# One gated-recurrence attention and max-of-two MLP kernel: two stages in sequence rewritten as one software pipeline by groups of 512 tokens

## The chip, the cores and the metric

The kernel runs on one core of one Trainium2 chip. The metric is the device time of a run in microseconds (us); before the change the median of three runs is 328.61 us (328.46 to 329.25).

## The reference

Attention: for 4 batches, 8 heads, 768 positions and a head size of 48, a 48x48 state is decayed and updated at each position, and the output reads it.

```python
f = 1.0 / (1.0 + np.exp(-f_logit))
for t in range(S):
    state = f[:, :, t, :, None] * state + np.einsum('bhd,bhe->bhde', k[:, :, t], v[:, :, t])
    y[:, :, t] = np.einsum('bhd,bhde->bhe', q[:, :, t], state)
x = attn_out.transpose(0, 2, 1, 3).reshape(B * S, H * D)      # 3072 tokens x 384
h1 = x @ w1                                                   # w1, w2: 384 x 1024
h2 = x @ w2
out = np.maximum(h1, h2) @ w_out                              # w_out: 1024 x 384
```

## The kernel before

The recurrence is computed in chunks of 128 positions. An outer loop runs over the 6 chunks, an inner one over the 4 batches, so there are 24 steps, and a step handles 128 tokens of all 8 heads. In a step, three DMAs on SyncE (SP) and one on GpSimd (POOL, with a cast to bf16; line 81) bring q, k, f and v in runs of 48 numbers. ScalarE (ACT) makes `ell = ln(1 + exp(-f))` (lines 90 and 91). TensorE (PE) sums it along the chunk with a triangular matrix (`cumL`, line 94) and per head (line 112). ACT takes two exponentials of the sums (lines 98 and 99) and one of the totals (line 115). POOL scales q and k with them (lines 103 and 106). PE transposes both (lines 120 and 121), and VectorE (DVE) copies the transposes out in two pieces of 48 partitions, even and odd heads (lines 124 and 125). PE forms the 8 products of 128x128 (`at_all`, line 136), and DVE multiplies them with the triangular mask (line 138). PE applies them to v and adds the part of the state (`yps`, lines 143 and 144) and forms the state's increment (line 149), DVE makes the new state (lines 152 and 154), and ACT copies the output to `x_sbuf` (line 158).

After the 24 steps come the weights: three DMAs of 1.5 MB (lines 165 to 167), three casts on DVE (lines 171 to 173), and 72 transposes of `x_sbuf` with one DVE copy each (lines 182 and 183). Then, for 8 blocks of 128 hidden units and 6 groups of 512 tokens, PE makes `h1` and `h2` with three 512-column matmuls each (lines 196 and 199), ACT copies `h1` to bf16 (line 202) and DVE takes the maximum (line 203). At last 24 tiles of 128 tokens are multiplied with `w_out`, eight 384-column matmuls each (line 209), copied by DVE (line 212) and stored (line 213).

The order on each engine is made by the tile framework's scheduler: it may put an instruction of a later step ahead of a waiting one. Attention and weights have pools of their own, and in PSUM `h1` and `h2` have one buffer each. `gT` holds the maxima of all 3072 tokens.

Of the kernel before, what the change touches and what calls it, by code (L numbers as in the profile page):

```python
# [1 line left out]
logging.getLogger("concourse").setLevel(logging.ERROR)  # L2
# [8 lines left out]
F32 = mybir.dt.float32  # L11
BF16 = mybir.dt.bfloat16
AF = mybir.ActivationFunctionType
# [3 lines left out]
def kernel(  # L17
# [10 lines left out]
):  # L28
    nc = tc.nc
    B, H, S, D = q.shape  # L30
    C = 128
    nch = S // C
    dm = H * D
    d_ff = moe_w1.shape[1]
    n_tok = B * S
    DGRP = dm // C
    FGRP = d_ff // C
    HD = H * D
    DP = 64
    HDP = H * DP  # L40

    consts = ctx.enter_context(tc.tile_pool(name="consts", bufs=1))
    ut = consts.tile([C, C], BF16)
# [5 lines left out]
    ut_big = consts.tile([C, H, C], BF16)  # L49
    for h in range(H):  # L50
        nc.gpsimd.tensor_copy(ut_big[:, h, :], ut)  # L51

    n_tok_tiles = n_tok // C
    x_sbuf = consts.tile([C, n_tok_tiles, dm], BF16, name="x_sbuf")

    with ExitStack() as ast:
        attn_pool = ast.enter_context(tc.tile_pool(name="attn", bufs=2))
        fpool = ast.enter_context(tc.tile_pool(name="fpool", bufs=2))
        state_pool = ast.enter_context(tc.tile_pool(name="state", bufs=2))
        ps_cum = ast.enter_context(tc.tile_pool(name="ps_cum", bufs=1, space=bass.MemoryType.PSUM))  # L60
        ps_tr = ast.enter_context(tc.tile_pool(name="ps_tr", bufs=1, space=bass.MemoryType.PSUM))
        ps_at = ast.enter_context(tc.tile_pool(name="ps_at", bufs=2, space=bass.MemoryType.PSUM))
        ps_y = ast.enter_context(tc.tile_pool(name="ps_y", bufs=1, space=bass.MemoryType.PSUM))
        ps_sa = ast.enter_context(tc.tile_pool(name="ps_sa", bufs=1, space=bass.MemoryType.PSUM))

        states = []
        for b in range(B):
            st = state_pool.tile([D, H, D], BF16, name="state", tag=f"state{b}")
            nc.gpsimd.memset(st, 0.0)
            states.append(st)  # L70
        for c in range(nch):
            for b in range(B):
                state = states[b]
                qt = attn_pool.tile([C, H, D], F32, name="qt", tag="qt")
                kt = attn_pool.tile([C, H, D], F32, name="kt", tag="kt")
                vt = attn_pool.tile([C, H, D], BF16, name="vt", tag="vt")
                ft = attn_pool.tile([C, H, D], F32, name="ft", tag="ft")
                sl = slice(c * C, (c + 1) * C)
                nc.sync.dma_start(out=qt, in_=q[b, :, sl, :].rearrange("h p d -> p h d"))
                nc.sync.dma_start(out=kt, in_=k[b, :, sl, :].rearrange("h p d -> p h d"))  # L80
                nc.gpsimd.dma_start(out=vt, in_=v[b, :, sl, :].rearrange("h p d -> p h d"))  # L81
                nc.sync.dma_start(out=ft, in_=f_logit[b, :, sl, :].rearrange("h p d -> p h d"))
                q_c = qt.rearrange("p h d -> p (h d)")
                k_c = kt.rearrange("p h d -> p (h d)")
                v_c = vt.rearrange("p h d -> p (h d)")
                ft2 = ft.rearrange("p h d -> p (h d)")

                ell_c = attn_pool.tile([C, HD], BF16, name="ell_c", tag="ell_c")
                tmp = attn_pool.tile([C, HD], F32, name="tmpf", tag="tmpf")
                nc.scalar.activation(tmp, ft2, AF.Exp, bias=0.0, scale=-1.0)  # L90
                nc.scalar.activation(ell_c, tmp, AF.Ln, bias=1.0, scale=1.0)  # L91

                cumL = ps_cum.tile([C, HD], F32, name="cumL")
                nc.tensor.matmul(out=cumL, lhsT=ut, rhs=ell_c, start=True, stop=True)  # L94

                F_dec = fpool.tile([C, HD], F32, name="F_dec", tag="F_dec")
                F_inv = fpool.tile([C, HD], F32, name="F_inv", tag="F_inv")
                nc.scalar.activation(F_dec, cumL, AF.Exp, bias=0.0, scale=-1.0)  # L98
                nc.scalar.activation(F_inv, cumL, AF.Exp, bias=0.0, scale=1.0)

                qp = fpool.tile([C, HDP], BF16, name="qp", tag="qp")
                kp = fpool.tile([C, HDP], BF16, name="kp", tag="kp")
                nc.gpsimd.tensor_mul(qp.rearrange("p (h e) -> p h e", h=H)[:, :, :D],  # L103
                                     q_c.rearrange("p (h d) -> p h d", h=H),
                                     F_dec.rearrange("p (h d) -> p h d", h=H))
                nc.gpsimd.tensor_mul(kp.rearrange("p (h e) -> p h e", h=H)[:, :, :D],  # L106
                                     k_c.rearrange("p (h d) -> p h d", h=H),
                                     F_inv.rearrange("p (h d) -> p h d", h=H))

                ell_sum = ps_sa.tile([D, HD], F32, name="ell_sum", tag="sa")[:, :H]  # L110
                for j in range(H):
                    nc.tensor.matmul(out=ell_sum[:, j:j + 1], lhsT=ell_c[:, j * D:(j + 1) * D],
                                     rhs=ones_col, start=True, stop=True)
                F_last = fpool.tile([D, H], F32, name="F_last", tag="F_last")
                nc.scalar.activation(F_last, ell_sum, AF.Exp, bias=0.0, scale=-1.0)

                trq = ps_tr.tile([C, 2 * HDP], BF16, name="trq")
                npiece = HDP // C
                for p in range(npiece):
                    nc.tensor.transpose(out=trq[:, p * C:(p + 1) * C], in_=qp[:, p * C:(p + 1) * C], identity=ident)  # L120
                    nc.tensor.transpose(out=trq[:, HDP + p * C:HDP + (p + 1) * C], in_=kp[:, p * C:(p + 1) * C], identity=ident)  # L121
                trSe = fpool.tile([D, 2 * HDP], BF16, name="trSe", tag="trSe")
                trSo = fpool.tile([D, 2 * HDP], BF16, name="trSo", tag="trSo")
                nc.vector.tensor_copy(trSe, trq[0:D, :])  # L124
                nc.vector.tensor_copy(trSo, trq[64:64 + D, :])

                def head_slice(base, j):
                    p = j // 2
                    t = trSe if (j % 2) == 0 else trSo
                    return t[:, base + p * C:base + (p + 1) * C]  # L130
                qpT = lambda j: head_slice(0, j)
                kpT = lambda j: head_slice(HDP, j)

                at_all = ps_at.tile([C, H, C], F32, name="at_all")
                for j in range(H):
                    nc.tensor.matmul(out=at_all[:, j, :], lhsT=kpT(j), rhs=qpT(j), start=True, stop=True)  # L136
                at_m = fpool.tile([C, H, C], BF16, name="at_m", tag="at_m")
                nc.vector.tensor_mul(at_m, at_all, ut_big)  # L138

                yps = ps_y.tile([C, HD], F32, name="yps")  # L140
                for j in range(H):
                    ds = slice(j * D, (j + 1) * D)
                    nc.tensor.matmul(out=yps[:, ds], lhsT=at_m[:, j, :], rhs=v_c[:, ds], start=True, stop=False)  # L143
                    nc.tensor.matmul(out=yps[:, ds], lhsT=qpT(j), rhs=state[:, j, :], start=False, stop=True)  # L144

                sadd = ps_sa.tile([D, HD], F32, name="sadd", tag="sa").rearrange("d (h e) -> d h e", h=H)
                for j in range(H):
                    kps = kp[:, j * DP:j * DP + D]
                    nc.tensor.matmul(out=sadd[:, j, :], lhsT=kps, rhs=v_c[:, j * D:(j + 1) * D], start=True, stop=True)  # L149

                tmpS = fpool.tile([D, H, D], F32, name="tmpS", tag="tmpS")
                nc.vector.tensor_add(tmpS, state, sadd)  # L152
                new_state = state_pool.tile([D, H, D], BF16, name="state", tag=f"state{b}")
                nc.vector.tensor_mul(new_state, tmpS, F_last.to_broadcast([D, H, D]))
                states[b] = new_state

                ti = b * nch + c
                nc.scalar.copy(x_sbuf[:, ti, :], yps)  # L158

    with ExitStack() as mst:  # L160
        wpool = mst.enter_context(tc.tile_pool(name="wpool", bufs=1))
        w1_f = wpool.tile([C, DGRP, d_ff], F32, name="w1_f")
# [81 lines left out]
```

## Time and profile before

| what | value |
|---|---|
| median of 3 runs | 328.61 us |
| span of the profiled execution, first to last instruction | 324.3 us |
| outside the span, median less span | 4.3 us |
| PE busy, share of the span | 253.9 us, 78% |
| DVE | 155.3 us, 48% |
| ACT | 148.7 us, 46% |
| POOL | 75.2 us, 23% |
| DMA, mean over the span | 81 GB/s |

For the profiled execution only its span is given, so its own time is taken as the span with the same 4.3 us around it. A busy share is a mean over stretches that differ: attention fills the first 193 us, weights and transposes the next 19, the two hidden products the next 81, and the output product the last 31. Matmuls overlap, and the end of each is modelled, so that a busy PE is not a PE at its peak; what one matmul costs in a stream is read from the distance between starts.

### The profile page before, as it was taken

To read this page: it belongs to the slowest core of one execution; us is meant where nothing else is said; L and a number is where in the kernel's file an instruction comes from. 1 tells how busy PE (TensorE), PEld (TensorE's weight loads), DVE (VectorE), ACT (ScalarE), POOL (GpSimd) and SP (SyncE) were. 2 spreads that over 40 slices of the span, in tenths; PEclk is the share of its full clock that TensorE was granted. 3 is DMA by queue.
4 is the path that set the end of the run, shared out by engine and by line. 5 is a ranking of instruction groups with operands and counts; after the bars stand their busy time and mean duration, and the time that the engine had idled before them with its cause. 6 is when DMAs were issued, how large, how long until landed. Compare 5 with 4: busy or idle time off the path is not lost.

```text
span 324.3 us, 4531 instructions
## 1 busy us (share of the span) xinstructions
PE 253.9 (78%) x1728; PEld 150.3 (46%) x1728; DVE 155.3 (48%) x267; ACT 148.7 (46%) x241; POOL 75.2 (23%) x93
## 2 busy tenths in 40 slices
PE   0258857967867697789879787688999998999995
PEld 0136635644555365456546554333333333345663
DVE  0145443645545365564546638934444444444442
ACT  3973668467927965784687010023333333330000
POOL 6353235432433351364434200000000000000000
PEclk9999999999999999999999999999999999999999
DMA  9947465856665687667674209500000000012443
GB/s 147 120 80 114 51 87 78 142 63 85 98 99 73 79 117 111 85 89 114 90 99 25 14 8 379 196 2 0 0 0 2 0 0 0 2 50 97 161 157 121
DMA packets 105156, 26.23 MB, mean 81 GB/s; under 512 B 100272, under 2 KB 104368, under 8 KB 105136
## 3 DMA queue, kind: packets, MB, share of 16 engines
q1 hardware_dynamic: 80176, 23.60, 31.8%
q0 software_dynamic: 24960, 2.36, 13.9%
q8 instruction: 13, 0.21, 0.3%
q14 instruction: 7, 0.06, 0.1%
HBM read 23.59 MB, written 4.72 MB: 87 GB/s over the span
## 4 chain that ended last, share of the span: by engine, by line
issue 37%; PE 30%; POOL 17%; DVE 12%; ACT 2%; DMA 1%; DVEq 0%; POOLq 0%; ACTq 0%
PE h L199 12%; PE ops L209 10%; DVE gT L203 8%; POOL kp L106 7%; POOL vt L81 6%; POOL qp L103 3%; PE h L196 3%; PE tps L182 2%; DVE xT L183 2%; PE yps L143 1%; PE yps L144 1%; DMA vt<-in_v_dram 1%; ACT L91 1%; POOL ut_big L51 1%; DVE wo L173 1%
## 5 line engine op out<-in xcount | busy, mean ns | idle before, releaser
L202 ACT CAST gT<-h 128x512 bf16<-128x512 f32 x48 | 28.1, 585 | 71.1 <-PE h L196 71.1
L203 DVE TENSOR_TENSOR gT<-gT,h 128x512 bf16<-128x512 bf16 x48 | 33.0, 687 | 48.0 <-PE h L199 48.0
L138 DVE TENSOR_TENSOR at_m<-at_all,ut_big 128x1024 bf16<-128x1024 f32 x24 | 29.4, 1224 | 43.7 <-PE at_all L136 43.7
L199 PE MATMUL h<-xT,w 128*128 128x512 bf16 x144 | 39.5, 382 | 7.4 <-DVE gT L203 7.4
L143 PE MATMUL yps<-vt,at_m 128*128 128x48 bf16 x192 | 42.8, 223 | 1.3 <-DVE at_m L138 1.3
L103 POOL TENSOR_TENSOR qp<-qt,F_dec 128x384 bf16<-128x384 f32 x24 | 23.7, 988 | 72.6 <-ACT F_dec L98 69.9
L196 PE MATMUL h<-xT,w 128*128 128x512 bf16 x144 | 39.8, 387 | 0.3 <-DVE xT L183 0.3
L94 PE MATMUL cumL<-ell_c,ut 128*128 128x384 bf16 x24 | 11.7, 487 | 30.1 <-ACT ell_c L91 25.5
L158 ACT CAST x_sbuf<-yps 128x384 bf16<-128x384 f32 x24 | 11.5, 477 | 50.0 <-PE yps L144 49.6
L209 PE MATMUL ops<-wo,gT 128*128 128x384 bf16 x192 | 33.2, 326 | 0.0
L91 ACT ACT_TABLE_LOAD x24 | 30.8, 1283 | 0.4
L81 POOL DMA_DIRECT2D vt<-in_v_dram x24 | 22.6, 941 | 34.5 <-PE yps L144 31.1
L149 PEld LDWEIGHTS <-kp 128*48 128x48 bf16 x192 | 9.7, 128 | 44.0 <-DMA vt<-in_v_dram 35.4
L124 DVE COPY trSe<-trq 48x1024 bf16<-48x1024 bf16 x24 | 16.4, 681 | 25.9 <-PE trq L121 25.9
L199 PEld LDWEIGHTS <-w 128*128 128x128 bf16 x144 | 14.1, 98 | 29.9 <-issue 18.4
L121 PE MATMUL trq<-ident,kp 128*128 128x128 bf16 x96 | 25.0, 313 | 3.2 <-POOL kp L106 3.2
L149 PE MATMUL sadd<-vt,kp 128*48 128x48 bf16 x192 | 12.7, 217 | 18.7 <-DMA vt<-in_v_dram 18.0
L143 PEld LDWEIGHTS <-at_m 128*128 128x128 bf16 x192 | 20.1, 105 | 12.0 <-DVE at_m L138 1.6
L106 POOL TENSOR_TENSOR kp<-kt,F_inv 128x384 bf16<-128x384 f32 x24 | 25.4, 1056 | 0.1
L152 DVE TENSOR_TENSOR tmpS<-state,sadd 48x384 f32<-48x384 bf16 x24 | 13.1, 546 | 25.1 <-PE sadd L149 24.9
L209 PEld LDWEIGHTS <-gT 128*128 128x128 bf16 x192 | 18.8, 98 | 13.7
L120 PE MATMUL trq<-ident,qp 128*128 128x128 bf16 x96 | 24.1, 303 | 0.0
(42 smaller groups left out, 370.6 us busy)
## 6 DMA issues: line engine op xcount, KB each, us to landing
qt<-in_q_dram SPq DMA_DIRECT2D x24, 192.0 KB, 2.7
kt<-in_k_dram SPq DMA_DIRECT2D x24, 192.0 KB, 3.2
ft<-in_f_logit_dram SPq DMA_DIRECT2D x24, 192.0 KB, 3.7
out_dram<-obuf SPq DMA_DIRECT2D x24, 192.0 KB, 1.9
w_f<-in_moe_w_dram SPq DMA_DIRECT2D x2, 1536.0 KB, 8.4
vt<-in_v_dram POOLq DMA_DIRECT2D x24, 96.0 KB, 3.7
wo_f<-in_moe_w_out_dram SPq DMA_DIRECT2D x1, 1536.0 KB, 14.1
```

The costliest lines, as they stand in the source:

```text
L81: nc.gpsimd.dma_start(out=vt, in_=v[b, :, sl, :].rearrange("h p d -> p h d"))
L91: nc.scalar.activation(ell_c, tmp, AF.Ln, bias=1.0, scale=1.0)
L103: nc.gpsimd.tensor_mul(qp.rearrange("p (h e) -> p h e", h=H)[:, :, :D], q_c.rearrange("p (h d) -> p h d", h=H), F_dec.rearrange("p (h d) - ...
L106: nc.gpsimd.tensor_mul(kp.rearrange("p (h e) -> p h e", h=H)[:, :, :D], k_c.rearrange("p (h d) -> p h d", h=H), F_inv.rearrange("p (h d) - ...
L121: nc.tensor.transpose(out=trq[:, HDP + p * C:HDP + (p + 1) * C], in_=kp[:, p * C:(p + 1) * C], identity=ident)
L138: nc.vector.tensor_mul(at_m, at_all, ut_big)
L143: nc.tensor.matmul(out=yps[:, ds], lhsT=at_m[:, j, :], rhs=v_c[:, ds], start=True, stop=False)
L196: nc.tensor.matmul(out=h1, lhsT=w1[:, j, ffb * C:(ffb + 1) * C], rhs=xT[:, j, tslice], start=(j == 0), stop=(j == DGRP - 1))
L199: nc.tensor.matmul(out=h2, lhsT=w2[:, j, ffb * C:(ffb + 1) * C], rhs=xT[:, j, tslice], start=(j == 0), stop=(j == DGRP - 1))
L202: nc.scalar.copy(gslc, h1)
L203: nc.vector.tensor_max(gslc, gslc, h2)
L209: nc.tensor.matmul(out=ops, lhsT=gT[:, ffb, i * C:(i + 1) * C], rhs=wo[:, ffb, :], start=(ffb == 0), stop=(ffb == FGRP - 1))
```

## The change

The schedule is written out by hand (`manual_schedule`: each engine runs its instructions in the order of the program), and the two stages are one loop. Step i of the loop, from -4 to 23, holds five stages of attention for different steps: output and state of step i (`s_y`), transposes of step i+2, products of i+1, cumulative sums of i+3, transposes of the output of i (`s_xT`), and the logarithms of i+4 (`s_ell`). Between them stand "units" from a queue: first 21 units that prepare the weights, then, for each group of 4 steps (512 tokens, one chunk of the four batches), 8 units `u_d` and 8 half-tiles `u_o`, which are queued when the group's fourth step ends.

The maximum is rewritten: max(h1, h2) = h2 + relu(h1 - h2). So the output is relu(x (w1 - w2)) w_out + x (w2 w_out). The weights' difference `wd` and the product `w2o` = w2 w_out (384x384) are made once; a tile of 128 tokens then needs 3 matmuls with `w2o` and 8 with `w_out`, and the product with w2, ACT's copy and DVE's maximum are gone; ACT takes a relu in their place.

ACT loads the table set named in the code ahead of the loop. All loads go through SP, v as f32 with a cast on DVE (`vb`); five steps of input buffers stand in place of two. Two heads share one padded 128-row operand, so the sums take 4 matmuls in place of 8, the increment 4 in place of 8, and the output product 12 in place of 16; DVE copies the transposes in one piece of 128 partitions. POOL makes the new state in two pieces of 64 partitions.

```diff
+    ctx.enter_context(tc.manual_schedule())
...
+    loads = ctx.enter_context(tc.tile_pool(name="loads", bufs=5))
...
+    ps_s = ctx.enter_context(tc.tile_pool(name="ps_s", bufs=3, space=bass.MemoryType.PSUM))
+    ps_a = ctx.enter_context(tc.tile_pool(name="ps_a", bufs=1, space=bass.MemoryType.PSUM))
+    ps_m = ctx.enter_context(tc.tile_pool(name="ps_m", bufs=3, space=bass.MemoryType.PSUM))
...
+    nc.scalar.preload_act_table_set("natural_log_exp_and_others")
...
+    def load(i):
...
+        for name, src in (("f", f_logit), ("k", k), ("q", q), ("v", v)):
+            t[name] = loads.tile([C, H, D], F32, name=f"{name}t", tag=f"{name}t")
+            nc.sync.dma_start(out=t[name], in_=src[b, :, sl, :].rearrange("h p d -> p h d"))
...
+    for i in range(3):
+        load(i)
+    nc.sync.dma_start(out=w2_f, in_=moe_w2.rearrange("(j p) ff -> p j ff", p=C))
+    nc.sync.dma_start(out=wo_f, in_=moe_w_out.rearrange("(j p) dm -> p j dm", p=C))
+    load(3)
+    nc.sync.dma_start(out=w1_f, in_=moe_w1.rearrange("(j p) ff -> p j ff", p=C))
+    load(4)
...
+    def u_w2_cast(j):
+        nc.vector.tensor_copy(w2_h[:, j, :], w2_f[:, j, :])
...
+    def u_wo_cast(h):
+        s = slice(h * 2, h * 2 + 2)
+        nc.scalar.copy(wo[:, s, :], wo_f[:, s, :])
...
+    def u_wd(j):
+        nc.vector.tensor_sub(wd[:, j, :], w1_f[:, j, :], w2_f[:, j, :])
...
+    def u_w2T(f):
+        ps = ps_m.tile([C, JG, C], BF16, name="w2tp", tag="mm")
+        for j in range(JG):
+            nc.tensor.transpose(out=ps[:, j, :], in_=w2_h[:, j, f * C:(f + 1) * C], identity=ident)
+        nc.vector.tensor_copy(w2T[:, f, :], ps.rearrange("p j c -> p (j c)"))
...
+    def u_w2o(j):
+        ps = ps_m.tile([C, dm], F32, name="w2op", tag="mm")
+        for f in range(FG):
+            nc.tensor.matmul(out=ps, lhsT=w2T[:, f, j * C:(j + 1) * C], rhs=wo[:, f, :],
+                             start=(f == 0), stop=(f == FG - 1))
+        nc.scalar.copy(w2o[:, j, :], ps)
...
+        def u_d(f):
+            ps = ps_m.tile([C, GT], F32, name="d", tag="mm")
+            for j in range(JG):
+                nc.tensor.matmul(out=ps, lhsT=wd[:, j, f * C:(f + 1) * C], rhs=xT[:, j, :],
+                                 start=(j == 0), stop=(j == JG - 1))
+            nc.scalar.activation(gT[:, f, :], ps, AF.Relu)
...
+        def u_o(b, half):
...
+            mms = [(xT[:, j, ts], w2o[:, j, :]) for j in range(JG)]
+            mms += [(gT[:, f, ts], wo[:, f, :]) for f in range(FG)]
+            cut = 6
+            todo = range(0, cut) if half == 0 else range(cut, len(mms))
...
+            if half == 1:
+                ob = work.tile([C, dm], F32, name="ob", tag="ob", bufs=3)
+                nc.vector.tensor_copy(ob, ps)
...
+    def s_ell(i):
...
+        nc.scalar.activation(e, t["f"].rearrange("p h d -> p (h d)"), AF.Exp, scale=-1.0)
+        nc.scalar.activation(ell[:, :, 0:D], e.rearrange("p (h d) -> p h d", h=H), AF.Ln, bias=1.0)
...
+        nc.vector.tensor_copy(vb, t["v"].rearrange("p h d -> p (h d)"))
...
+    def s_cum(i):
...
+        nc.tensor.matmul(out=ps[:, 0:dm], lhsT=ut, rhs=ell[:, :, 0:D], start=True, stop=True)
+        for p in range(NP):
+            nc.tensor.matmul(out=ps[:, dm + p:dm + p + 1],
+                             lhsT=ell[:, 2 * p:2 * p + 2, :].rearrange("p h d -> p (h d)"),
+                             rhs=ones_col, start=True, stop=True)
...
+        nc.scalar.activation(ei, ps[:, 0:dm], AF.Exp)
+        nc.scalar.activation(ed, ps[:, 0:dm], AF.Exp, scale=-1.0)
+        nc.scalar.activation(fl, ps[:, dm:dm + NP], AF.Exp, scale=-1.0)
...
+        nc.gpsimd.tensor_mul(kp[:, :, 0:D], t["k"], ei.rearrange("p (h d) -> p h d", h=H))
+        nc.gpsimd.tensor_mul(qp[:, :, 0:D], t["q"], ed.rearrange("p (h d) -> p h d", h=H))
...
+    def s_tr(i):
...
+        nc.vector.tensor_copy(tr, ps)
...
+    def s_a(i):
...
+                r = slice(o * DP, o * DP + D)
+                nc.tensor.matmul(out=ps[:, o, p, :], lhsT=tr[r, 0, p, :], rhs=tr[r, 1, p, :],
+                                 start=True, stop=True)
...
+    def s_y(i):
...
+        if c < nch - 1:
+            sa = ps_s.tile([C, NP, 2 * D], F32, name="sa", tag="s")
...
+            nc.vector.tensor_add(tmp, sa, old)
...
+                nc.gpsimd.tensor_mul(new[r, :, e], tmp[r, :, e],
+                                     s["fl"][r, :].unsqueeze(2).to_broadcast([DP, NP, D]))
...
+        nc.scalar.copy(x, y)
...
+    def s_xT(i):
...
+        nc.vector.tensor_copy(xT_g[c][:, :, b * C:(b + 1) * C], ps)
...
+    for i in range(-4, T):
+        if i >= 0:
+            s_y(i)
+        unit()
+        if 0 <= i + 2 < T:
+            s_tr(i + 2)
+        unit()
+        if 0 <= i + 1 < T:
+            s_a(i + 1)
+        unit()
+        if 0 <= i + 3 < T:
+            s_cum(i + 3)
+        unit()
+        if i >= 0:
+            s_xT(i)
+        if i < B:
+            unit()
+            unit()
+        if i >= 0 and i % B == B - 1:
+            push_group(i // B)
+        if 0 <= i + 4 < T:
+            s_ell(i + 4)
+        if 5 <= i + 8 < T:
+            load(i + 8)
+    while units:
+        unit()
```

All removed lines are those of the kernel before, shown above: its attention loop, its weight stage and its two product stages as wholes.

## Rows read from the trace of the kernel before

**Rows 1.** Windows: busy time and count of each engine, granted clock, DMA share, GB/s.

```profile
core 0: us, PE busy (x) PEld busy (x) DVE busy (x) ACT busy (x) POOL busy (x), PEclk, DMA share, GB/s
0.00:193.00 193.00, 139.74 (x1176) 95.73 (x1176) 92.52 (x120) 120.11 (x192) 75.21 (x93) 1.00 0.64 87
193.00:212.00 19.00, 12.95 (x73) 7.60 (x73) 16.63 (x75) 0.48 (x1) 0.00 (x0) 1.00 0.68 249
212.00:293.00 81.00, 73.54 (x311) 30.50 (x312) 33.27 (x50) 28.09 (x48) 0.00 (x0) 1.00 0.02 6
293.00:324.30 31.30, 27.65 (x170) 16.42 (x168) 12.87 (x23) 0.00 (x0) 0.00 (x0) 1.00 0.38 139
```

**Rows 2.** Waits over the span: who waited for whom, total us, times, longest.

```profile
POOL qp L103 <- ACT F_dec L98: 69.9, 21, 5.5
ACT x_sbuf L158 <- PE yps L144: 49.6, 20, 5.6
DVE at_m L138 <- PE at_all L136: 43.7, 23, 2.7
```

**Rows 3.** Timeline of PE in attention: start, duration, instruction.

```profile
13.32 0.31 PE L120 MATMUL trq<-ident,qp 128*128 128x128 bf16 x1
...
14.07 0.31 PE L121 MATMUL trq<-ident,kp 128*128 128x128 bf16 x1
...
132.62 0.31 PE L136 MATMUL at_all<-trSo 48*128 48x128 bf16 x1
...
132.87 0.29 PE L120 MATMUL trq<-ident,qp 128*128 128x128 bf16 x1
```

**Rows 4.** Timeline of PE in the two product stages, streams merged (last: their count).

```profile
213.32 1.49 PE L199 MATMUL h<-xT,w 128*128 128x512 bf16 x3
214.60 1.14 PE L196 MATMUL h<-xT,w 128*128 128x512 bf16 x3
...
250.50 0.81 PE L199 MATMUL h<-xT,w 128*128 128x512 bf16 x3 [0.20 <-DVE gT L203]
...
251.14 0.81 PE L196 MATMUL h<-xT,w 128*128 128x512 bf16 x3
...
313.82 6.83 PE L209 MATMUL ops<-wo,gT 128*128 128x384 bf16 x41
```

**Rows 5.** Groups by line, ACT: count, busy us, mean ns, idle before.

```profile
L91 ACT ACT_TABLE_LOAD x24 | 30.8, 1283 | 0.4
L98 ACT ACT_TABLE_LOAD x16 | 20.5, 1283 | 4.7 <-PE cumL L94 4.3
L91 ACT ACTIVATE ell_c<-tmpf 128x384 bf16<-128x384 f32 x24 | 12.5, 522 | 0.3
L98 ACT ACTIVATE F_dec<-cumL 128x384 f32<-128x384 f32 x24 | 11.7, 486 | 1.0 <-PE cumL L94 0.8
L158 ACT CAST x_sbuf<-yps 128x384 bf16<-128x384 f32 x24 | 11.5, 477 | 50.0 <-PE yps L144 49.6
L202 ACT CAST gT<-h 128x512 bf16<-128x512 f32 x48 | 28.1, 585 | 71.1 <-PE h L196 71.1
```

**Rows 6.** Groups by line, POOL and DVE, the same columns.

```profile
L106 POOL TENSOR_TENSOR kp<-kt,F_inv 128x384 bf16<-128x384 f32 x24 | 25.4, 1056 | 0.1
L138 DVE TENSOR_TENSOR at_m<-at_all,ut_big 128x1024 bf16<-128x1024 f32 x24 | 29.4, 1224 | 43.7 <-PE at_all L136 43.7
L124 DVE COPY trSe<-trq 48x1024 bf16<-48x1024 bf16 x24 | 16.4, 681 | 25.9 <-PE trq L121 25.9
L152 DVE TENSOR_TENSOR tmpS<-state,sadd 48x384 f32<-48x384 bf16 x24 | 13.1, 546 | 25.1 <-PE sadd L149 24.9
L212 DVE COPY obuf<-ops 128x384 f32<-128x384 f32 x24 | 13.3, 557 | 15.1 <-PE ops L209 14.2 <-DMA out_dram<-obuf 0.8
L171 DVE CAST w<-w_f 128x3072 bf16<-128x3072 f32 x1 | 1.8, 1750 | 0.0
```

**Rows 7.** Windows of two stretches in which the DMA engines were full.

```profile
2.00:7.00 5.00, 0.00 (x0) 0.00 (x0) 0.00 (x0) 0.84 (x3) 3.98 (x12) 1.00 1.12 201
196.00:206.00 10.00, 6.88 (x38) 4.00 (x38) 8.93 (x39) 0.00 (x0) 0.00 (x0) 1.00 1.03 403
```

**Rows 8.** Timeline: the last instruction on DVE before the span ends.

```profile
320.68 0.56 DVE L212 COPY obuf<-ops 128x384 f32<-128x384 f32 x1 [0.74 <-PE ops L209]
```

More of the change, by code (lines that the diff above doesn't have):

```diff
@@ L2 @@
 logging.getLogger("concourse").setLevel(logging.ERROR)
+from collections import deque
 from contextlib import ExitStack
@@ L48 @@
     nc.gpsimd.memset(ones_col, 1.0)
[L49 to L66, printed above, removed]
-        for b in range(B):
[L68 to L158, printed above, removed]
@@ new lines @@
+    mask = consts.tile([C, H, C], BF16, name="mask")
+    nc.vector.tensor_copy(mask, ut.unsqueeze(1).to_broadcast([C, H, C]))
+    w2_h = consts.tile([C, JG, d_ff], BF16, name="w2_h")
+    wd = consts.tile([C, JG, d_ff], BF16, name="wd")
+    wo = consts.tile([C, FG, dm], BF16, name="wo")
+    w2T = consts.tile([C, FG, dm], BF16, name="w2T")
+    w2o = consts.tile([C, JG, dm], BF16, name="w2o")
+    units = deque()
+    def u_w2_cast(j):
+        nc.vector.tensor_copy(w2_h[:, j, :], w2_f[:, j, :])
@@ new lines, in unit @@
+    def unit(n=1):
+        for _ in range(n):
+            if units:
+                units.popleft()()
+    st = {}
+    def s_ell(i):
+        t = ld[i]
+        e = work.tile([C, dm], F32, name="e", tag="e")
+        ell = ell_b[i % 2]
+        nc.scalar.activation(e, t["f"].rearrange("p h d -> p (h d)"), AF.Exp, scale=-1.0)
+        nc.scalar.activation(ell[:, :, 0:D], e.rearrange("p (h d) -> p h d", h=H), AF.Ln, bias=1.0)
+        vb = work.tile([C, dm], BF16, name="vb", tag="vb", bufs=6)
+        nc.vector.tensor_copy(vb, t["v"].rearrange("p h d -> p (h d)"))
+        st[i] = {"ell": ell, "v": vb}
@@ new lines, in s_tr @@
+    def s_tr(i):
+        s = st[i]
+        ps = ps_s.tile([C, 2, NP, C], BF16, name="tr", tag="s")
+        for n, src in enumerate((s["kp"], s["qp"])):
+            for p in range(NP):
+                nc.tensor.transpose(out=ps[:, n, p, :],
+                                    in_=src[:, 2 * p:2 * p + 2, :].rearrange("p h d -> p (h d)"),
+                                    identity=ident)
+        tr = work.tile([C, 2, NP, C], BF16, name="trs", tag="trs", bufs=3)
+        nc.vector.tensor_copy(tr, ps)
+        s["tr"] = tr
@@ new lines, in s_a @@
+    def s_a(i):
+        s = st[i]
+        tr = s["tr"]
+        ps = ps_a.tile([C, 2, NP, C], F32, name="a", tag="a")
+        for p in range(NP):
+            for o in range(2):
+                r = slice(o * DP, o * DP + D)
+                nc.tensor.matmul(out=ps[:, o, p, :], lhsT=tr[r, 0, p, :], rhs=tr[r, 1, p, :],
+                                 start=True, stop=True)
+        am = work.tile([C, 2, NP, C], BF16, name="am", tag="am")
+        nc.vector.tensor_mul(am.rearrange("p o n c -> p (o n) c"),
+                             ps.rearrange("p o n c -> p (o n) c"), mask)
+        s["am"] = am
@@ new lines, in s_xT @@
+    def s_xT(i):
+        c, b = divmod(i, B)
+        s = st.pop(i)
+        if b == 0:
+            xT_g[c] = work.tile([C, JG, GT], BF16, name="xT", tag="xT", bufs=3)
+        ps = ps_s.tile([C, JG, C], BF16, name="xtp", tag="s")
+        for j in range(JG):
+            nc.tensor.transpose(out=ps[:, j, :], in_=s["x"][:, j * C:(j + 1) * C], identity=ident)
+        nc.vector.tensor_copy(xT_g[c][:, :, b * C:(b + 1) * C], ps)
[23 more added lines that the diff above has]
+            load(i + 8)
```

141 lines of the change are left out of this document (87 added, 54 removed).

## The prediction

> **What bounds the kernel now.** I read the windows by stretch first, then the waits, the groups by line, and last the timeline of PE, to see what one matmul costs in a stream. The windows show four stretches of 193, 19, 81 and 31 us [rows 1]. The reader is to see that no engine is full in the first: of 193 us PE is busy 140, ACT 120, DVE 93, POOL 75, DMA 64%. A step of attention takes about 7.7 us there, and the waits say why: POOL waits 70 us for ACT's exponentials, ACT 50 us for the output of PE, DVE 44 us for the products [rows 2]. It is a chain from engine to engine with little laid beside it. In the third and fourth stretch PE is busy 74 of 81 and 28 of 31 us [rows 1] and sets the pace, while POOL and DMA stand still. So one stretch has PE to spare and the others have nothing but PE: laid side by side they could fill it, and what then counts is the sum of PE's work.
>
> PE's price per matmul differs between the stretches. Eight transposes start 0.107 us apart (13.32 to 14.07, seven distances) [rows 3]: 128 columns at 1.2 GHz. The first 512-column products start 1.28/3 = 0.427 us apart, which is 1.2 GHz too, and later ones 0.64/3 = 0.213, which is 2.4 GHz; 384 columns then take (6.83 - 0.33)/40 = 0.163 [rows 4]. The granted clock reads 1.00 in all four stretches [rows 1], so the column doesn't show this, the distances do: attention and the transposes ran at the lower level, and the clock rose about 3 us into the dense products.
>
> **The change part by part.** I cost the steady step first (steps 4 to 23), then start and end.
>
> *PE, one step.* Attention issues 39 matmuls and transposes with a 128-row or padded weight load (4 sums, 8 transposes, 8 products, 4 increments, 12 for the output, 3 transposes of the output) and one of 384 columns. At the lower clock a piece is 0.107 [rows 3]: 39 x 0.107 + 0.32 = 4.5 us. At the higher clock no row shows it. Half, 0.053, bounds it from below and 0.107 from above (the loading of weights may not follow the clock); I take the middle, 0.08: 39 x 0.08 + 0.16 = 3.3 us. The products cost, per group of four steps, 24 matmuls of 0.213 and 44 of 0.163 [rows 4], 12.3 us, or 3.1 a step. Changing between kinds (48 rows, transposes, plain) costs 0.25 in place of 0.107 where the products end and transposes begin [rows 3], so 0.14 more; six changes a step are 0.4 to 0.8, I take 0.5. Sum 6.9 us a step. With both bounds: 2.2 + 3.1 + 0.4 = 5.7, and 4.3 + 3.1 + 0.8 = 8.2.
>
> *The removed product.* h2's 144 matmuls and DVE's 48 maxima go, 144 x 0.213 = 31 us of PE; 72 matmuls with w2o at 0.163 (11.7 us) come in, with 24 transposes and 24 matmuls of preparation (6 to 10 us). The 0.20 us that PE waited for the maximum in each pair [rows 4] goes too: three buffers stand in place of one.
>
> *ACT.* Two table loads a step go, 24 + 16 of those shown at 1.28 us and nine more on two other lines [rows 5], 63 us in all. Left are per step two activations of 0.52, two of 0.49, a small one, the copy of 0.48 and on average two relus of about 0.585 [rows 5]: 3.8 us, under PE's 6.9.
>
> One rule prices the switches higher. The Trainium skill, "ScalarE: Activation LUTs", section "What ACT_TABLE_LOAD costs", adds a drain and comes to about 2.66 us for each switch, by which the 49 would be 130 us; here the 24 logarithms waited 0.3 us in all beyond their loads of 1.28 [rows 5], so the trace disagrees. The sum uses neither, since ACT isn't what ends the new step.
>
> *DVE, POOL, DMA.* DVE per step: 0.68 for the copy of the transposes (one in place of two), 1.22 for the mask, 0.55 for the increment, and at most 0.56 each for the output's transposes, the cast of v and the output tile [rows 6]: 4.1 at most. POOL: two products of 1.06 [rows 6] and two half-size pieces of the new state, not shown before, between half of 1.06 and all of it: 3.2 to 4.2. It loses the loads of v, and with them the place where its queue waited. DMA: four loads of 0.197 MB at 201 GB/s, 0.98 us each, and a store at 403, 0.5 [rows 7]: 4.4. All stay under 6.9, so the step is PE's, if the handovers fit. The tightest: from the sums to the transposes of the same step lie ACT's 0.49, POOL's 2 x 1.06 and handovers, 2.8 us; PE has a unit, the output's transposes, the next step's output and another unit in between, 0.7 + 0.25 + 1.3 + 0.7 = 2.95. It just fits. On SP a load stands behind the store of an output tile and that behind its copy; loads are issued four steps ahead of use, some 27 us, so this costs nothing until they are that late. On ACT the exponential of f waits for its load, and behind it stands the next copy of an output, which PE's transposes wait for: covered by the same 27 us.
>
> *Start.* Everything now goes through SP's one queue: 12 small loads of 0.98 from about 2 us on, then w2 and w_out, 1.57 MB each at 403, 3.9 us [rows 7]: w_out is there at about 22.5. Three casts of w_out stand on ACT ahead of the first exponential, 0.8 each (from 0.585 for 512 columns and 0.48 for 384 [rows 5]), so the first logarithm ends near 26; on PE the transposes of w2 stand ahead of the first sums and wait for w2 too, which lands earlier. Then sums, exponentials and POOL's two products (4 us, to 30), the rest of w2's transposes and 24 matmuls for w2o, 3.9 at the higher and 7.7 at the lower clock (to 36), and the first output with the waits on the way (step 0 ends near 44). Steps 1 to 3 have no units; their chain is about 4.7 each, PE's 4.5 at the lower clock being the most of it: step 4 starts at 58, between 50 and 65.
>
> *End.* The last chunk needs no new state: 4 x 4 matmuls, -1.4 us. After step 23 the last group's 16 units stand alone, 12.3 us, then the last copy, 0.56, and 3.1 to the end of the span as before (321.24 to 324.3 [rows 8]): 16.
>
> *Sum.* 58 + 20 x 6.9 - 1.4 + 16 = 210.6 of span; 4.3 lie between span and median, taken the same here: **215 us**. With the bounds of the step and the start it is 183 to 248; PE's pieces are more likely near the middle than at either end, so I give the case itself 196 to 236.
>
> **The rivals.**
>
> *The clock stays at 1.2 GHz.* For it: it did in all of attention, though PE was busy 140 of 193 us [rows 1], and the mixed step has the same transposes and small pieces. Against: dense products of 512 columns raised it within 3 us [rows 4], and at the lower level the mixed step would leave PE no idle time. The step is 4.5 + 0.8 + 6 x 0.427 + 11 x 0.32 = 11.4 us, the last group 24.3: 58 + 228 - 1.4 + 28 + 4.3 = 317 us. A clock that goes up and down lies between.
>
> A rule speaks for this. The Trainium skill, "TensorE: Matmul & The Clock Gate", section "A second HAM failure mode: psum-queue depth-cycling", says that short PE pauses between matmul groups in cycling PSUM buffers can make the clock swing, and "Part 4: PE-mode transpose" that the full clock does not engage for transposes. No row here shows a mixed stream; the 0.20 us pauses of the third stretch didn't lower it.
>
> *Handovers set the step.* The margin above is 0.15 us; POOL and DVE can slow each other, and in strict program order one late instruction holds all behind it. With 0.5 us lost at three places (transposes, mask, relu) the step is 8.4: 58 + 168 + 14.6 + 4.3 = 245 us.
>
> *The table loads stay.* Were two still made per step, ACT would need 3.8 + 2.6 = 6.4 us, on the tight handover as well; step about 8, 237 us.
>
> *Slower: strict order lays the step end to end.* If each stage waits for the one before it, the step is sums 0.6, exponentials 1.0, POOL 2.1, transposes 0.85, copy 0.7, products 0.85, mask 1.2, output 1.7, copy 0.5, transposes 0.3 and copy 0.4, 10.2, and units 3.1: 13.3 us, and 58 + 266 + 14.6 + 4.3 = 343 us. It decides from (328.6 - 77)/20 = 12.6 us a step. Against it: stages that follow each other in the program belong to different steps, and no wait of rows 2 is longer than 5.6 us.
>
> **How the numbers follow.** The forecast has 0.62, handovers 0.16, the lower clock or a swinging one 0.14, the table loads 0.03, the slower one 0.04, anything else 0.01. The range is 196 to 262: it holds the forecast, the handovers, the loads and the mildest swings, and leaves out the clock at its worst, the slower case and a step below 5.9 us, about 0.2. A measurement of this kernel tells a change of 0.3%, 1 us. Faster has 0.95 (all but the slower case and a clock with further stalls), same 0.01, slower 0.04.
>
> **What would show it.** Right: PE busy over 85% from 60 us on; 512-column products 0.21 apart inside the mixed steps; a period of 6.5 to 7.3; one table load; the first exponential near 25 us. Wrong: 0.427 between products in the mixed steps (the clock); PE waiting for POOL's qp or DVE's mask (handovers); ACT waiting for f's load, which would make DMA the bound; attention pieces well off 0.08.

## The result, and the profile after

The changed kernel takes 185.62 us (median of 4 runs, 185.37 to 186.78) against 328.65 us: a ratio of 0.566, with a 95% interval of 0.564 to 0.568. The forecast was 215 us with a range of 196 to 262. The direction and most of the mechanism were right; the time lies 10 us below the range, because the price of the small pieces on PE was too high.

The windows of the changed kernel at the three joints of the forecast, start, mixed steps and end (columns as in [rows 1]):

```profile
0.00:58.50 58.50, 24.49 (x235) 16.70 (x236) 30.23 (x48) 20.36 (x48) 23.14 (x40) 0.84 1.17 223
58.50:163.20 104.70, 98.09 (x1048) 59.96 (x1058) 68.48 (x108) 60.54 (x146) 52.57 (x68) 0.99 0.67 135
163.20:183.60 20.40, 16.05 (x92) 8.72 (x90) 3.80 (x8) 5.21 (x9) 0.00 (x0) 0.99 0.19 69
```

The start ends at 58.5 as worked out (58). The windows above end the mixed steps at the last copy of an output, 163.2; two output tiles that the forecast counted to step 23 stand behind it, and the step ends with the transposes of its output (timeline of PE after):

```profile
166.48 0.33 PE L290 MATMUL xtp<-ident,x 128*128 128x128 bf16 x3
167.56 5.34 PE L156 MATMUL d<-xT,wd 128*128 128x512 bf16 x23 [0.74 <-DVE xT L291]
```

In the forecast's own terms the mixed steps so take 108.1 us (58.5 to 166.6) in place of 136.6, and the end 17.0 in place of 16. Outside the span lie 1.8 us in place of 4.3: this execution took 185.38 us for a span of 183.6, and a later run of the kernel before has 328.03 for 326.2. By that the profiled execution of the kernel before was some 2.5 us quicker than the median, and the 4.3 was too large by as much. The error of 29.5 us for this execution is the mixed steps' -28.5, with +0.5, +1.0 and -2.5 beside it. PE is busy 98 of the 104.7 us: it is nearly full, as the forecast said, only with less work than it was given.

Step by step, ACT's copies of the output show the period (timeline of ACT after, one copy a step; some of them stand here):

```profile
59.43 0.48 ACT L280 CAST x<-y 128x384 bf16<-128x384 f32 x1
...
82.14 0.46 ACT L280 CAST x<-y 128x384 bf16<-128x384 f32 x1
...
104.43 0.46 ACT L280 CAST x<-y 128x384 bf16<-128x384 f32 x1
...
143.26 0.46 ACT L280 CAST x<-y 128x384 bf16<-128x384 f32 x1
149.01 0.46 ACT L280 CAST x<-y 128x384 bf16<-128x384 f32 x1
...
163.16 0.48 ACT L280 CAST x<-y 128x384 bf16<-128x384 f32 x1 [4.07 <-PE y L277]
```

Four steps take 22.3 us, one 5.57, where 6.9 was forecast. The last four, steps 20 to 23, take 19.9 (143.26 to 163.16), since the stages for later steps run out; the forecast had taken only the state's matmuls off there.

One whole step on PE (timeline after; it answers to [rows 3] and [rows 4]):

```profile
97.46 0.33 PE L290 MATMUL xtp<-ident,x 128*128 128x128 bf16 x3
97.63 0.33 PE L260 MATMUL sa<-vb,kp 128*128 128x96 bf16 x4
97.87 0.20 PE L272 MATMUL y<-st,trs 128*128 128x96 bf16 x1
97.91 0.21 PE L277 MATMUL y<-vb,am 128*128 128x48 bf16 x2
...
98.25 0.65 PE L172 MATMUL o<-w2o,xT 128*128 128x384 bf16 x3
98.73 0.65 PE L172 MATMUL o<-wo,gT 128*128 128x384 bf16 x3
99.22 0.39 PE L230 MATMUL tr<-ident,kp 128*128 128x128 bf16 x4
99.66 0.40 PE L230 MATMUL tr<-ident,qp 128*128 128x128 bf16 x4
99.90 0.98 PE L172 MATMUL o<-wo,gT 128*128 128x384 bf16 x5
100.80 0.40 PE L245 MATMUL a<-trs 48*128 48x128 bf16 x8
101.13 0.66 PE L172 MATMUL o<-w2o,xT 128*128 128x384 bf16 x3
...
102.12 0.33 PE L208 MATMUL cum<-ell,ut 128*128 128x384 bf16 x1
102.28 0.24 PE L210 MATMUL cum<-ones_col,ell 128*128 128x1 bf16 x4
102.39 0.97 PE L172 MATMUL o<-wo,gT 128*128 128x384 bf16 x5
103.19 0.33 PE L290 MATMUL xtp<-ident,x 128*128 128x128 bf16 x3
```

From start to start the attention pieces of this step take 0.17, 0.24, 0.38 (98.25 - 97.87), 0.68, 0.33 and 0.27: 2.07 us, where the forecast had 3.3 for the pieces and 0.5 for changes of kind. In the 2.07 are two waits, 0.22 between the two groups of transposes and 0.08 ahead of the output. The units take what was forecast: three of 384 columns 0.48, 0.16 each. The eight products start 0.024 apart ((0.40 - 0.23)/7, with 0.23 for one), the transposes 0.056, the four sums 0.024, the twelve of the output 0.032. All but the transposes lie under the bound of 0.053 that the forecast set for a piece. A change of kind costs time at one place only, around the products, the pieces with weights of 48 rows: the matmul ahead of them takes 0.26 from start to start in place of 0.16, and the last of them 0.15 in place of 0.05, so each of the two turns costs about 0.1. Between transposes and plain matmuls of 128 rows nothing is added.

The waits after, of PE and ACT, over the whole span:

```profile
ACT wo L116 <- DMA wo_f<-in_moe_w_out_dram: 21.9, 1, 21.9
...
PEld L230 <- POOL qp L221: 10.0, 22, 1.4
...
PE y L272 <- ACT fl L218: 2.7, 9, 0.4
```

ACT stands 21.9 us for w_out at the start, as forecast. The handover that PE waits for in nearly every step is the tight one: POOL's product ahead of the transposes. A second wait stands ahead of the output, in the steps with `u_d`. The profile puts it down to ACT's last exponential (`fl`), the last reader of the sums. Sums and output come from one pool of three PSUM buffers, so it is likely a buffer that the output waits for; no run with a fourth one shows it.

### The profile page after: what moved, and what is told of

The parts are those of the page before. It is cut to its first block, busy times and chain, and to the rows that moved or that the text cites. A ratio compares the mean times of both kernels' runs of the same rounds, so it can differ in the third digit from the quotient of the medians.

```text
span 183.6 us, 3633 instructions
## 1 busy us (share of the span) xinstructions
PE 138.6 (75%) x1373; PEld 85.4 (46%) x1384; DVE 102.5 (56%) x161; ACT 86.1 (47%) x200; POOL 75.7 (41%) x107
## 4 chain that ended last, share of the span: by engine, by line
issue 39%; PE 32%; POOL 23%; ACT 3%; POOLq 1%; DVE 1%; ACTq 0%
PE o L172 13%; POOL qp L221 11%; POOL kp L220 9%; PE d L156 9%; PE tr L230 6%; PE a L245 2%; POOL st L98 1%; ACT ei L216 1%; PE y L272 1%; ACT ed L217 1%; PE y L277 1%; ACT gT L158 1%; POOLq L345 1%; POOL ell L94 0%; PE cum L208 0%
## 5 line engine op out<-in xcount | busy, mean ns | idle before, releaser
L220 POOL TENSOR_TENSOR kp<-kt,ei 128x384 bf16<-128x384 f32 x24 | 24.9, 1036 | 76.4 <-issue 38.9
L156 PE MATMUL d<-xT,wd 128*128 128x512 bf16 x133 | 36.7, 383 | 2.3 <-DVE xT L291 1.1
L158 ACT ACTIVATE gT<-d 128x512 bf16<-128x512 f32 x48 | 29.0, 605 | 19.0 <-PE d L156 18.5
L172 PE MATMUL o<-wo,gT 128*128 128x384 bf16 x192 | 37.7, 326 | 0.0
L234 DVE COPY trs<-tr 128x1024 bf16<-128x1024 bf16 x24 | 16.6, 692 | 25.8 <-PE tr L230 25.7
L248 DVE TENSOR_TENSOR am<-a,mask 128x1024 bf16<-128x1024 f32 x24 | 29.3, 1219 | 2.9 <-PE a L245 2.9
L221 POOL TENSOR_TENSOR qp<-qt,ed 128x384 bf16<-128x384 f32 x24 | 27.6, 1148 | 0.0
L267 POOL TENSOR_TENSOR st<-tmp,fl 64x192 bf16<-64x192 f32 x40 | 20.0, 501 | 2.3 <-DVE tmp L264 0.8
L201 DVE CAST vb<-vt 128x384 bf16<-128x384 f32 x24 | 16.9, 703 | 0.0
L172 PE MATMUL o<-w2o,xT 128*128 128x384 bf16 x72 | 15.7, 327 | 0.0
L116 ACT CAST wo<-wo_f 128x768 bf16<-128x768 f32 x4 | 3.1, 824 | 21.9 <-DMA wo_f<-in_moe_w_out_dram 21.9
```

The costliest lines, as they stand in the source:

```text
L156: nc.tensor.matmul(out=ps, lhsT=wd[:, j, f * C:(f + 1) * C], rhs=xT[:, j, :], start=(j == 0), stop=(j == JG - 1))
L158: nc.scalar.activation(gT[:, f, :], ps, AF.Relu)
L172: nc.tensor.matmul(out=ps, lhsT=mms[n][0], rhs=mms[n][1], start=(n == 0), stop=(n == len(mms) - 1))
L201: nc.vector.tensor_copy(vb, t["v"].rearrange("p h d -> p (h d)"))
L220: nc.gpsimd.tensor_mul(kp[:, :, 0:D], t["k"], ei.rearrange("p (h d) -> p h d", h=H))
L221: nc.gpsimd.tensor_mul(qp[:, :, 0:D], t["q"], ed.rearrange("p (h d) -> p h d", h=H))
```

## The experiments

**The changed kernel again**, beside the next three on one chip.

> The changed kernel itself, unchanged, as the measure for its neighbours on the same chip: 185 to 187 us, and a mixed step of 5.4 to 5.7 us.

Measured 186.26 us, ratio 0.568 (0.567 to 0.570).

**Two row groups.** The products read partitions 0 to 47 and 64 to 111 in turn; here both read 0 to 47.

```diff
-                r = slice(o * DP, o * DP + D)
+                r = slice(0, D)
```

> The 8 products of a step take the even heads twice, so that all read partitions 0 to 47; the odd heads' products are left out. Theory 1 (a small piece costs its moving columns at the higher clock, weight loads are hidden, and two row groups run side by side): the 8 products start 0.053 us apart in place of 0.024, 0.24 us more a step, 189 to 192 us. Theory 2 (padding and row groups are what made the pieces cheap; without them they go back to 0.107): 0.65 us more a step, 198 to 202 us.

Measured 191.97 us, 5.7 more, as theory 1 said. Timeline of PE in this kernel:

```profile
104.20 0.62 PE L245 MATMUL a<-trs 48*128 48x128 bf16 x8
104.75 0.66 PE L172 MATMUL o<-w2o,xT 128*128 128x384 bf16 x3
```

(0.62 - 0.23)/7 = 0.056 in place of 0.024: 128 columns at 2.4 GHz. Two row groups at once halve the price. That is the rule of the Trainium skill, "TensorE: Matmul & The Clock Gate", section "Part 3: Packing small matmuls", that matmuls in distinct row groups run concurrently; the trace agrees (0.024 against 0.056).

**The state's part in 48 rows.**

```diff
+            for o in range(2):
...
+                if c > 0:
+                    nc.tensor.matmul(out=y[:, ds], lhsT=tr[0:D, 1, p, :],
+                                     rhs=old[0:D, p, 0:D], start=False, stop=True)
```

> The state's part of the output is made again by 8 matmuls with weights of 48 rows, in turn with the 128-row ones, as in the kernel before (the odd heads take the even heads' part). Theory 1: 4 more pieces at 0.024 to 0.035, 0.1 to 0.15 us a step, 187 to 190 us. Theory 2: the pieces go back to the 0.15 us that they were apart in the kernel before, or half of it at the higher clock: 0.8 us or more a step, 200 us or more.

Measured 212.88 us, 26.6 more: theory 1 fails here. Timeline of PE, the first three of the sixteen and what follows them:

```profile
100.33 0.18 PE L274 MATMUL y<-vb,am 128*128 128x48 bf16 x1 [0.27 <-DVE xT L291]
100.44 0.19 PE L277 MATMUL y<-st,trs 48*128 48x48 bf16 x1
100.57 0.20 PE L274 MATMUL y<-vb,am 128*128 128x48 bf16 x1
...
102.35 0.66 PE L172 MATMUL o<-w2o,xT 128*128 128x384 bf16 x3
```

Sixteen pieces take 2.02 us, 0.126 each, where twelve took 0.38. Both kinds have 48 columns, 0.02 us at 2.4 GHz, so about 0.1 us of each piece is the turn from 128-row weights to 48-row ones or back, the price that the changed kernel pays twice a step around its products. It costs a step 1.6 us on PE; the run pays 1.3 a step, since the wait between the transposes goes. The weight loads in the same stretch, and one of the changed kernel:

```profile
100.56 0.10 PEld L274 LDWEIGHTS <-am 128*128 128x128 bf16 x1
100.69 0.09 PEld L277 LDWEIGHTS <-trs 48*128 48x128 bf16 x1
...
97.94 0.10 PEld L272 LDWEIGHTS <-trs 128*128 128x128 bf16 x1
```

At a turn a load starts 0.12 us after the piece before it, right ahead of its own matmul (100.56 and 100.57). In the changed kernel the load at 97.94 starts together with the piece before, and its matmul follows at 97.97. So the 0.1 stands ahead of the load; the load's own 0.09 overlaps its matmul in both.

**Without the common table set.**

```diff
-    nc.scalar.preload_act_table_set("natural_log_exp_and_others")
```

> Only the line that loads the common table set is taken out. Theory 1: two loads a step come back, ACT then has 3.8 + 2.6 = 6.4 us a step against PE's 5.4 and sets the step, 20 to 30 us more: 205 to 215 us. Theory 2: ACT has room beside PE, and the loads hide: 186 to 190 us.

Measured 219.69 us, 33.4 more, above what theory 1 gave. Groups by line, ACT:

```profile
L198 ACT ACT_TABLE_LOAD x24 | 30.8, 1283 | 0.5
L215 ACT ACT_TABLE_LOAD x24 | 30.8, 1283 | 18.3 <-PE cum L209 18.1
```

The window of 70 to 160 us:

```profile
70.00:160.00 90.00, 68.70 (x715) 41.54 (x719) 44.67 (x77) 73.87 (x128) 35.55 (x49) 0.96 0.66 137
```

Two loads a step are back. ACT is busy 74 of 90 us and PE 69: neither is full. So theory 1 had the direction, but not the cause: ACT doesn't set the step by its share. The waits in the same window show what does:

```profile
PE y L271 <- ACT fl L217: 18.3, 13, 1.8
```

One of the two loads stands on ACT between the sums and the exponentials that read them, and PE waits ahead of the output for the last of these: 1.4 us in each of 13 steps, where the changed kernel has 2.7 us in 9 over its whole span. A step takes 6.82 us in place of 5.57. For POOL's product, ahead of the transposes, PE waits only 1.2 us in this window. About 10 of the 33 us fall on the start, where step 4's copy comes at 69.45 in place of 59.43. The rule of the Trainium skill, "ScalarE: Activation LUTs", section "Table sets: the hidden batching unit", that one set holds both exponential and logarithm, agrees: 49 loads here, the 48 above and one at the start, and one in the changed kernel.

The next three runs are a set of their own, in which the kernel before took 326.32 us; what they add is taken from the ratios to it, times 327.

**The stages in sequence.** No units from step 0 to 23.

```diff
-            if units:
+            if units and not 0 <= now["i"] < T:
```

> No units between the stages of attention from step 0 on: all products of the MLP run after step 23 (six buffers for the group's inputs in place of two and three). Theory 1 (PE stays at the lower clock without the dense products, and a step of attention alone is 4.5 us, as in steps 0 to 3): 58 + 20 x 4.5 + 6 x 12.3 + 8 = 230 us, 224 to 236, clock 0.50 through attention. Theory 2 (algebra, table set and shorter steps are the gain, the order adds nothing): 186 to 192 us.

Measured 222.73 us, ratio 0.684 (0.682 to 0.686) against 0.568: 38 us more, a little under theory 1. Windows, attention and products:

```profile
58.00:140.00 82.00, 60.27 (x731) 47.65 (x728) 64.07 (x91) 41.30 (x107) 51.35 (x68) 0.54 0.81 130
145.00:215.00 70.00, 69.74 (x377) 37.46 (x381) 11.90 (x22) 27.62 (x47) 0.00 (x0) 0.99 0.16 60
```

The granted clock is 0.54 in attention, 0.50 being the lower level, and 0.99 in the products; in the mixed steps above it is 0.99 throughout. For a short time it rises in attention, twice, so that two neighbouring steps show both levels (timeline of PE):

```profile
86.03 0.28 PE L274 MATMUL y<-st,trs 128*128 128x96 bf16 x1
...
86.69 0.60 PE L232 MATMUL tr<-ident,kp 128*128 128x128 bf16 x4
87.09 0.63 PE L232 MATMUL tr<-ident,qp 128*128 128x128 bf16 x4
...
90.20 0.21 PE L274 MATMUL y<-st,trs 128*128 128x96 bf16 x1
...
90.64 0.38 PE L232 MATMUL tr<-ident,kp 128*128 128x128 bf16 x4
```

The twelve pieces of the output take 0.66 us at the lower level and 0.44 at the higher, 0.055 and 0.037 apiece, counted to the start of the transposes. They have 768 columns together (4 x 96 + 8 x 48): 0.64 at 1.2 GHz, 0.32 at 2.4. With uniform 128-row weights a piece costs little more than its columns.

The clock is not the whole of the 38 us. PE is busy only 60 of the 82 us of attention. A step takes 4.43 us, and in 1.1 of them PE waits for ACT's `fl`, by the profile, here ahead of the output's transposes (16.3 us, 15 times). So theory 1's 4.5 a step came out without being PE's work. Around each of the two rises two steps take 8.43 and 8.53 us in place of 8.86; by an estimate from these a step wholly at the higher level would gain about 0.5 us, twenty of them some 10 of the 38. The larger part is idle time of PE that the products fill in the mixed steps. No run holds the clock and changes the order alone.

**The maximum back.** Two products, copy and maximum as before, inside the pipeline; wd is w1.

```diff
-            nc.scalar.activation(gT[:, f, :], ps, AF.Relu)
+            nc.scalar.copy(gT[:, f, :], ps)
...
+            nc.vector.tensor_max(gT[:, f, :], gT[:, f, :], ps2)
```

> The maximum is taken again from two products (copy on ACT, maximum on DVE), inside the new pipeline; the 21 preparing units become 10. Theory 1 (PE sets the step): 24 more matmuls of 0.213 and 12 fewer of 0.163 a group, 0.8 us a step, less 5 us of preparation at the start: 196 to 202 us. Theory 2 (waits set the step, PE has room): 181 to 188 us. A third, DVE as the bound at 3.6 + 1.4 us plus waits: over 205 us.

Measured 196.44 us, ratio 0.602 (0.600 to 0.604): 11 us more, as PE's sum said (the product with w2 and the smaller preparation together).

**Early attention.**

```diff
-    for i in range(3):
+    for i in range(4):
         load(i)
...
-    load(3)
-    nc.sync.dma_start(out=w1_f, in_=moe_w1.rearrange("(j p) ff -> p j ff", p=C))
     load(4)
...
-            if units:
+            if units and now["i"] >= 0:
...
+        if i == -2:
+            nc.sync.dma_start(out=w1_f, in_=moe_w1.rearrange("(j p) ff -> p j ff", p=C))
```

> The inputs of four steps are loaded ahead of the weights, w1 later still, and the 21 preparing units stand in steps 0 to 3 in place of steps -4 to -1. Theory 1 (the 58 us before the first mixed step are the wait for w_out and a chain at the lower clock; the mixed steps are PE's): the mixed steps start near 47 to 50 us, the rest is unchanged, 174 to 179 us. Theory 2 (DMA sets the whole, and what the start gains is given back by later waits for loads): 183 to 187 us.

Measured 179.24 us, ratio 0.550 (0.548 to 0.552): 6 us less, at the weak edge of theory 1.

The next five ran on two more chips (the kernel before: 327.07 for four of them, 327.47 for the last).

**Sums first.**

```diff
-        if 0 <= i + 2 < T:
-            s_tr(i + 2)
+        if 0 <= i + 3 < T:
+            s_cum(i + 3)
         unit()
         if 0 <= i + 1 < T:
             s_a(i + 1)
         unit()
-        if 0 <= i + 3 < T:
-            s_cum(i + 3)
+        if 0 <= i + 2 < T:
+            s_tr(i + 2)
```

> Only the order of three stages in a step is changed: the cumulative sums of step i+3 come first, then the products of i+1, then the transposes of i+2. Theory 1 (PE is full but for the handover from the sums over ACT and POOL to the transposes, 10 us of waits in 22 steps): that wait goes, 177 to 181 us. Theory 2 (the wait is only moved, the next handover is late by as much): 184 to 188 us.

Measured 173.84 us, ratio 0.531 (0.530 to 0.532): 12 us less than the changed kernel, more than theory 1 gave. Timeline of PE in it:

```profile
99.76 0.39 PE L230 MATMUL tr<-ident,kp 128*128 128x128 bf16 x4
99.98 0.39 PE L230 MATMUL tr<-ident,qp 128*128 128x128 bf16 x4
100.21 0.81 PE L156 MATMUL d<-xT,wd 128*128 128x512 bf16 x3
```

The second four start 0.22 us after the first, where they stood 0.44 apart: no wait is left between them, and none is left ahead of the output either. A mixed step takes 5.17 us (20.7 in four). The forecast had given this handover 0.15 us to spare and cost it at nothing.

Some 8 of the 12 us come from the mixed steps and 4 from the start, where step 4's copy comes at 55.05 in place of 59.43. Steps 1 to 3 have no units, and both kernels run them at a granted clock of 0.50. The output of steps 2 and 3 on PE, in sums first and then in the changed kernel:

```profile
47.54 0.48 PE L277 MATMUL y<-vb,am 128*128 128x48 bf16 x8 [0.31 <-DVE trs L234]
50.88 0.48 PE L277 MATMUL y<-vb,am 128*128 128x48 bf16 x8 [0.31 <-DVE trs L234]
...
49.56 0.48 PE L277 MATMUL y<-vb,am 128*128 128x48 bf16 x8 [0.42 <-DVE xT L291]
54.07 0.48 PE L277 MATMUL y<-vb,am 128*128 128x48 bf16 x8 [0.42 <-DVE xT L291]
```

The same work takes 3.34 us a step in the one order and 4.51 in the other. So the 4.5 of the changed kernel is not what PE's pieces cost at the lower clock; it holds over a microsecond of waits.

**Later logarithms, and the combinations.** The first moves `s_ell` of step i+3 to the head of step i, on top of the early attention; then early attention with sums first; then all three.

```diff
+        if 0 <= i + 3 < T:
+            s_ell(i + 3)
         if i >= 0:
             s_y(i)
...
-        if 0 <= i + 4 < T:
-            s_ell(i + 4)
```

> On top of the early attention: the logarithms of a step are made in the step of its sums, one step later than before, so that one load fewer has to land before the first mixed step. Theory 1 (DMA is full until the first mixed step and sets it): one load of 3.9 us less, 174 to 177 us. Theory 2 (the chain in a step, now longer by two activations, takes it back): 179 to 184 us.

> The early attention and the new order of the stages together. If the two gains are apart, one at the start and one in the mixed steps: 171 to 174 us. If the early start already took the handover wait: 178 to 180 us.

> Early attention, later logarithms and the new order of the stages together. If the three gains add: 167 to 171 us. If logarithms, sums and transposes in one step make a chain that PE waits for: 175 us or more.

Measured 179.45, 176.02 and 173.93 us, ratios 0.548, 0.537 (0.535 to 0.539) and 0.532 (0.530 to 0.535). On top of early attention alone, later logarithms give nothing. On top of early attention with sums first they give 2 us, with intervals that just don't meet; where, the two traces don't show, since both have the same long step. Early attention on top of sums first is 2 us slower than sums first alone, and all three together are no faster than sums first: 176.02 and 173.93 each lie between the two times that were forecast for them, so the gains add only in part. The chain of early attention with sums first shows where the gain went (start, duration, link):

```profile
71.49 3.66 DMA out_dram<-ob
```

And the timelines of DVE and of SP's queue in it:

```profile
65.08 0.56 DVE L174 COPY ob<-o 128x384 f32<-128x384 f32 x1 [1.63 <-PE o L170]
...
71.49 1.39 SPq L176 DMA_DIRECT2D out_dram<-ob  x2
...
75.27 0.56 DVE L174 COPY ob<-o 128x384 f32<-128x384 f32 x1 [2.21 <-DMA out_dram<-ob]
```

There are three tiles, so the copy at 75.27 waits for the store of the tile copied at 65.08. That store is issued only at 71.49, 5.8 us after its copy ended, behind loads in SP's queue, and takes 3.66 us to land. In sums first alone the same store goes out at 71.65, but the copy comes only at 67.45 and the next use of the tile finds it free. PE then waits 2.29 us for the copy that follows on DVE, and the clock falls: the next 512-column products start 0.43 us apart, and the granted clock is 0.83 in the window of 74 to 84 us. Step 9 takes 9.2 us.

**More output tiles.** Early attention and sums first, with eight output tiles.

```diff
-                ob = work.tile([C, dm], F32, name="ob", tag="ob", bufs=3)
+                ob = work.tile([C, dm], F32, name="ob", tag="ob", bufs=8)
```

> Early attention and the new order of the stages, with eight output tiles in place of three. Theory 1 (the one long pause left in the mixed steps, 9.2 us for step 9 against 5.2, is DVE's copy that waits for a store which stands in the DMA queue behind loads): with tiles to spare the pause goes, 171 to 173 us, below the new order alone. Theory 2 (DMA itself is the limit in this stretch, and the pause moves to a load): 175 to 177 us.

Measured 171.82 us, ratio 0.526 (0.523 to 0.530), 4 us less than with three tiles: theory 1, and step 9 takes 5.57 us. It is the lowest median of all, 14 us under the changed kernel; its interval just touches that of sums first alone, so the two are not told apart with certainty.

## Why the prediction was wrong

*The start* (58 us, of it the wait for w_out to about 22.5 and the lower clock): 58.5, ACT waiting 21.9 us, to 23.9. The wait and the lower level were right. That steps 1 to 3 took 4.5 each was luck: the forecast took PE's pieces for most of it, but PE was busy 10.5 of 13.5 us there, the rest were waits, and in sums first these steps take 3.34.

*PE sets the mixed step, the clock is up, one table load*: right. The rival of a clock at 1.2 GHz is out for this kernel: 0.99 is granted in the mixed steps, PSUM buffers cycling and transposes among the products. By the rule of the Trainium skill, "TensorE: Matmul & The Clock Gate", section "A second HAM failure mode: psum-queue depth-cycling", it might have swung; the windows disagree. The transposes too run at the higher level, 0.056 apart.

*The step that failed* is "39 matmuls and transposes" at a middle price of 0.08 with 0.5 for changes of kind, 3.8 us a step; over twelve steps (63.58 to 130.56 us) pieces and turns took 1.86, waits not counted. All 39 were priced as transposes of 128 columns, with a lower bound of 0.053, half of 0.107. But only 19 have 128 columns, and 8 of these go two at a time. A price per column would have had it: 8 x 128 transposes, 8 x 64, 4 x 96, 768 for the output, 3 x 128 and the sums' 384 are 3456 columns, 1.44 us at 2.4 GHz; the rest to 1.86 is the two turns at the products (0.2), the one-column sums at 0.024 each (0.1) and about 0.003 us that most pieces take beyond their columns. The 0.14 that the forecast read for a change of kind was that of 48-row products to 128-row transposes; it put it on six changes where two pay. The bound failed the same way, and the range with it. Both experiments on the form bear this out: one group costs what its columns say, and 0.126 apiece, dearer than my upper bound, comes back once 48-row and 128-row weights alternate, as the kernel before did. So the padding to uniform weights, which I costed only by counting pieces, is worth 26.6 us of the mixed kernel in the output alone. The forecast named "attention pieces well off 0.08" as a sign of being wrong, and it showed.

*Handovers*: named as tight at 0.15 us and put at nothing; over the same twelve steps PE waited 0.63 a step, 0.30 between the transposes for POOL's product, 0.26 ahead of the output and 0.07 ahead of `u_d`. With 1.86 + 3.09 for the units + 0.63 the measured 5.58 is accounted for. The tight handover failed by the same price: its chain took the 2.8 us that were forecast, but the work of PE laid over it was 2.56 in the step above (0.80 + 0.79 + 0.97) in place of 2.95, since the next step's output took 0.6 and not 1.3. Sums first, which takes the first two waits away, runs at 5.17.

*The last steps*: 19.9 us for steps 20 to 23 where 26.2 were forecast, 2.4 of the difference because the stages for later steps fall away (four at 5.57 are 22.3). *The end* was right within 1 us: PE waits 0.74 there for the last transposes of the output to be copied.

*Where the 143 us came from*, each part undone alone in the new kernel: order 38, table set 33, uniform weights in the output 27, the maximum 11, row groups 6. These overlap and don't sum to the whole; the five input buffers, the loads on one queue and the transposes' copy in one piece were not undone alone.

Not settled: why a weight load starts 0.1 us later at a turn. The traces show that the time lies ahead of the load and not in it; no run shows what it waits for.

## What to carry to other kernels

Price a small matmul by its moving columns at the clock that its stream will have, not by a count of pieces, and look for changes in the number of weight rows between neighbours: alternating 48 and 128 rows cost 0.1 us a piece, more than the work. Two phases laid side by side can pay twice: the dense one fills the waits of the sparse one, and it keeps the clock up for it; here the first seems the larger part. In a written-out order, place each stage so that the longest chain between engines has the most of the step behind it; moving three stages gave 12 us. And look at every wait of the engine that sets the pace, not only at the one that was named beforehand: here the second took 0.26 us a step beside the first's 0.30.

## What the runs showed of the hardware

The granted clock read 1.00 through the whole of the kernel before, though its matmuls started at the distances of 1.2 GHz in attention [rows 1, 3]; in the changed kernel it reads 1.00 until 40 us, then 0.50 until 60, though up to 33 us the transposes of w2 start 0.107 apart and the first matmuls of w2o 0.32, and only from 33 to 40 the latter start 0.163 apart. In these two traces the column's first 1.00 doesn't tell the level; distances between starts do.

A weight load of 128 columns cost nothing that shows where the weights keep their 128 rows: four sums of one moving column, each with new weights, start 0.024 us apart.
